# Linear attention and a GELU layer on one Trainium2 core: the order of all 3,662 operations comes from a table instead of a list scheduler

## The chip, the cores and the metric

The kernel runs on one core of a Trainium2 chip. A core has five engines, each of which takes its own instructions in order: TensorE (PE in the profile; its weight loads are shown as PEld), VectorE (DVE), ScalarE (ACT), GpSimd (POOL) and SyncE (SP, which issues nearly all DMA transfers). The metric is the device time of one execution in microseconds.

## The reference

```
def phi(x):
    proj = np.einsum('bhsd,df->bhsf', x, w_phi)
    proj = proj - np.max(np.abs(proj), axis=-1, keepdims=True)
    return np.concatenate([np.exp(proj), np.exp(-proj)], axis=-1)
q_p, k_p = (phi(q), phi(k))
kv = np.einsum('bhsf,bhsd->bhfd', k_p, v)
z = np.sum(k_p, axis=2)
num = np.einsum('bhsf,bhfd->bhsd', q_p, kv)
den = np.einsum('bhsf,bhf->bhs', q_p, z)[..., None] + 1e-06
x = (num / den), heads side by side: 4608 tokens x 512
h = x @ w_in                                          # 512 x 2048
out = (0.5 * h * (1.0 + erf(h / sqrt(2)))) @ w_out    # 2048 x 512
```

Batch and heads are 8 and 8, the sequence has 576 tokens, a head 64 numbers and 128 features. The weights of the layer arrive as float64.

## The kernel before, in words

**Attention** runs batch by batch (b = 0 to 7), two heads (a pair) at a time. `k_unit` and `k_quad` project keys on PE (tile `pk`, `pk_r` for the rest of a sequence), take the largest absolute value (`mx`, L465, DVE), subtract it (`ek` or `er`, L401, DVE) and exponentiate on ACT (L470); PE sums keys times values (`kv`), and ACT copies the sums out (`kvn`, L395). `q_pair` projects queries (`pq`), ACT copies them (`pc`), POOL finds the largest absolute value over the partitions (`mb`, L539), DVE subtracts it (`pc`, L401), ACT exponentiates twice (`ef`, L544), PE multiplies (`pn`, and for b under 3 the denominators `dn`), ACT copies the results (`xo`, `do`) and SP stores them. In what follows k10 is pair 0 of the keys of b = 1, and q001 is b = 0, pair 0, second half of the sequence; w_i0_0 and w_o1 are pieces of the two weights.

**Weights** are split from float64 into two float32r parts: 32 pieces of 128 x 512. Each piece (`split_weight`, L413 to L423) is a load of 512 KB (`raw`), an absolute value on ACT (L416, tile `wt`), four DVE instructions (L417, L419, L421, L423), a cast on ACT and a subtraction on DVE (L401, tile `w_i` or `w_o`).

**The layer** runs over 18 blocks of 256 tokens. `up` gives 12 matmuls per 128 hidden columns into `ph`; ACT applies GELU; DVE subtracts to get the low part (`gl`); the second product goes into `po`. Blocks 8 to 17 (`seven`) need fewer products (`pa`, `pb`).

All operations are recorded with `op` in `Plan.ops`, each with its engine, its dependencies and a rank. `Plan.order` then ran a list scheduler over them, with costs, latencies and a model of a few effects, and `emit` issued the operations by planned start. Tile places are fixed by name (`HOME`) and by each tag's own rotation. What counts on the chip is each engine's own sequence, since an engine never overtakes itself; SP's sequence is at once the order of the DMA transfers.

Of the kernel before, what the change touches and what calls it, by code (L numbers as in the profile page):

```python
# [62 lines left out]
class Plan:  # L63


    HOP = {"pe": 0.2, "act": 0.14, "dve": 0.13, "pool": 0.1, "sp": 0.05}
    SAME = {"pe": 0.0, "act": 0.0, "dve": 0.127, "pool": 0.1, "sp": 0.0}
    SWITCH = 1.3

    BEHIND = {"f": 0.1, "k": 0.1, "q": 0.095, "v": 0.09, "w": 0.09, "n": 0.1, "d": 0.05, "z": 0.09}  # L70
    BEFORE = {"f": 0.08, "k": 0.1, "q": 0.1, "v": 0.05, "w": 0.05, "n": 0.05, "d": 0.1, "z": 0.04}
    SHAPE = {"f": 0, "k": 1, "q": 1, "v": 2, "n": 2, "w": 3, "d": 4, "z": 5}
    READS = {"max": 1.15, "add": 2.45, "max main": 2.1, "add main": 4.43, "max rest": 1.05, "add rest": 2.15}
    WRITES = {"max": (1.4, 2.02), "add": (2.75, 3.47), "max main": (2.3, 3.42), "add main": (4.6, 5.97), "max rest": (1.2, 1.83), "add rest": (2.4, 3.1)}
    SPENT = {"max": 2.14, "add": 3.59, "max main": 3.54, "add main": 6.11, "max rest": 1.94, "add rest": 3.23}
    WINDOW = 3.413
    BUSY = 0.8
# [5 lines left out]

    def turn(self, a, b):
        return self.BEHIND[a] + self.BEFORE[b] + (0.09 if a == "f" and b != "d" else 0.0)

# [47 lines left out]
    def order(self, bias):  # L134
        free = dict(self.slots)
        slot_free_at = {t: [0.0] * n for t, n in self.slots.items()}
        turn = dict.fromkeys(self.slots, 0)
        engines = {}
        for o in self.ops:
            engines.setdefault(o.eng, [])  # L140
        clock = dict.fromkeys(engines, 0.0)
        table = [None]
        cand = {e: [] for e in engines}
        for o in self.ops:
            if o.wait == 0:
                cand[o.eng].append(o)
        done = []
        n = len(self.ops)

        gelus, left_at, dma, dge = [0], [0.0], [0.0], [0.9]  # L150
        port = [0.0]

        def start_of(o):
            t = max(clock[o.eng], o.ready)
            if o.table == "exp" and table[0] == "gelu" and gelus[0] % (2 * STICK):
                t = max(t, left_at[0] + PATIENCE)
            seen = {}
            for b in o.bufs:
                if not b.held and b.tag is not None:
                    f, i = slot_free_at[b.tag], seen.get(b.tag, 0)  # L160
                    if len(b.line) <= i or b.line[i] is not b:
                        return None
                    when = f[(turn[b.tag] + i) % len(f)]
                    if when is None:
                        return None
                    t = max(t, when)
                    seen[b.tag] = i + 1
            if o.eng == "dve":
                for a, z, least in port[1:]:
                    if o.port >= least and a <= t < z:  # L170
                        t = z
            return t


        clk = {"i": 0, "full": False, "busy": 0.0}
        last, first = ["f"], {}

        def run(t, work, duty):
            while work > 1e-9:
                i = int(t / self.WINDOW + 1e-9)  # L180
                while clk["i"] < i:
                    use = clk["busy"] / self.WINDOW
                    clk["full"] = use > (0.5 if clk["full"] else self.BUSY)
                    clk["i"] += 1
                    clk["busy"] = 0.0
                speed = 1.0 if clk["full"] else 0.51
                dt = min((i + 1) * self.WINDOW - t, work / speed)
                clk["busy"] += dt * duty
                work -= dt * speed
                t += dt  # L190
            return t

        while len(done) < n:
            best = None
            for e, lst in cand.items():
                if not lst:
                    continue
                opts = []
                for o in lst:
                    t = start_of(o)  # L200
                    if t is not None:
                        opts.append((t, o))
                if not opts:
                    continue
                t0 = min(t for t, _ in opts)
                lim = max(t0, clock[e]) + 0.02
                hold = 0.0
                if e == "pe" and last[0] == "f":
                    t_of = {id(o): max(o.ready, first.setdefault(o.n, t)) for t, o in opts}
                    there = [o for t, o in opts if t <= lim and o.kind != "f"]  # L210
                    if sum(o.cost for o in there) < LUMP and all(lim - t_of[id(o)] < LINGER for o in there):
                        hold = 4000.0
                key = None
                for t, o in opts:
                    if t <= lim:
                        k = o.rank
                        if e == "act" and o.table is not None and o.table != table[0]:
                            k += bias
                        if o.kind != "f":
                            k += hold  # L220
                        if key is None or (k, o.n) < key[0]:
                            key = ((k, o.n), t, o)
                if best is None or key[1] < best[1] or key[1] == best[1] and e == "pool":
                    best = key
            if best is None:
                raise RuntimeError("no operation can go")
            _, t, o = best
            cand[o.eng].remove(o)
            cost = o.cost
            if o.eng == "act" and o.table is not None and o.table != table[0]:  # L230
                cost += self.SWITCH
                table[0] = o.table
            if o.eng == "pe":
                if self.SHAPE[last[0]] != self.SHAPE[o.kind]:
                    cost += self.turn(last[0], o.kind)
                last[0] = o.kind
            o.start = t
            if o.eng == "pool" and o.port:
                t = max(t, port[0])
                a, z = self.WRITES[o.port]  # L240
                port[1:] = [(t, t + self.READS[o.port], 1), (t + a, t + z, 2)]
            o.end = run(t, cost, o.duty) if o.eng == "pe" else t + cost
            if o.nbytes:
                dge[0] = max(dge[0], t) + 0.55
                dma[0] = max(dma[0], dge[0] + 0.75) + o.nbytes / RATE
                o.late = dma[0] + 0.15 + DMASLACK - o.end
            if o.table == "gelu":
                gelus[0] += 1
                left_at[0] = o.end
            clock[o.eng] = o.end  # L250
            if o.eng == "dve" and o.port:
                port[0] = o.end
            for b in o.bufs:
                if b.tag is not None and not b.held:
                    f = slot_free_at[b.tag]
                    b.slot = turn[b.tag]
                    f[b.slot] = None
                    turn[b.tag] = (b.slot + 1) % len(f)
                    b.held = True
                    assert b.line.pop(0) is b  # L260
                b.left -= 1
                if b.left == 0 and b.tag is not None:
                    slot_free_at[b.tag][b.slot] = o.end + o.late + self.HOP[o.eng] + (PESLACK if b.tag in self.banks else 0.0)
            for u in o.users:
                u.wait -= 1
                u.ready = max(u.ready, o.end + o.late + (self.HOP if u.eng != o.eng else self.SAME)[o.eng] + (POOLSLACK if o.eng == "pool" else 0.0) + (PESLACK if u.eng == "pe" and o.eng != "pe" else 0.0))
                if u.wait == 0:
                    cand[u.eng].append(u)
            done.append(o)
        self.done = done  # L270
        return max(o.end + o.late for o in done)

    def emit(self):
        todo = sorted(self.done, key=lambda o: (o.start, o.n))
        parts = [o.part for o in todo if o.eng == "pe"][1:] + [None]
        for o in todo:
            if o.eng == "pe":
                self.then = parts.pop(0)
            if o.reopen and self.turn_over is not None:
                self.turn_over()  # L280
# [35 lines left out]
def fused_kernel(ctx: ExitStack, tc: tile.TileContext, qT, kT, va, w_st, w_in, w_out, out):  # L316
    nc = tc.nc
    plan = Plan(tc)
# [611 lines left out]
    total = plan.order(bias=BIAS)  # L930
# [155 lines left out]
```

## Time and profile before

| what | value |
|---|---|
| median of 3 runs | 1046.52 us (1044.51 to 1047.1) |
| profiled execution, its own time | 1048.43 us |
| span of its instructions | 1046.6 us |
| mean granted share of the TensorE clock | 0.993 |
| PE busy | 1019.6 us, 97% |
| DVE busy | 661.1 us, 63% |
| ACT busy | 614.5 us, 59% |
| POOL busy | 276.9 us, 26% |

Busy is the time in which an engine executes an instruction. Shares over the whole span hide stages: the page's 40 slices show DVE at nine tenths in the first eight slices and PE at nine tenths or more from the fifth on. A row of waits names who ended an idle stretch of an engine; a chain row is a piece of the path that ended last.

### The profile page before, as it was taken

The page shows a single profiled execution, that of the slowest core. Times are in us where ns is not written, and L with a number is a line of the kernel's source. Part 1 is how long each engine was busy: PE and PEld are TensorE (multiplying, and loading weights), DVE is VectorE, ACT ScalarE, POOL GpSimd, SP SyncE. Part 2 cuts the span into 40 slices and gives each one's busy share as a digit, 9 for nine tenths or more (in the row PEclk, how much of TensorE's full clock was granted, in tenths as well). Part 3 has the DMA queues.
Part 4 walks back from the last instruction along what each step waited for, and adds up shares of the span by engine and source line. Part 5 has one row for each costly group of instructions (what it writes and reads, how often), then busy time and mean ns, then how long its engine had stood idle before and what let it go on. Part 6 is the DMA issues. An engine that isn't in the chain of part 4 may idle for free.

```text
span 1046.6 us, 24197 instructions
## 1 busy us (share of the span) xinstructions
PE 1019.6 (97%) x10070; PEld 893.1 (85%) x10070; DVE 661.1 (63%) x1209; ACT 614.5 (59%) x1011; POOL 276.9 (26%) x72
## 2 busy tenths in 40 slices
PE   6889998999999999999999999999999999999998
PEld 5555776878878878897887889999999999999998
DVE  5899999987777854334643433555564556474754
ACT  5788888886768766757755642343243334243433
POOL 2343331373376352326566540000000000000000
PEclk9899999999999999999999999999999999999999
DMA  8775654524534433222321339201111111110000
GB/s 294 216 231 170 208 189 119 164 88 140 162 123 147 152 108 91 67 76 72 97 72 39 97 107 326 60 22 41 44 39 40 43 42 42 41 42 19 24 22 21
DMA packets 87327, 107.11 MB, mean 102 GB/s; under 512 B 29021, under 2 KB 57245, under 8 KB 87217
## 3 DMA queue, kind: packets, MB, share of 16 engines
q1 hardware_dynamic: 86928, 105.30, 32.7%
q8 instruction: 79, 1.29, 0.5%
q14 instruction: 32, 0.25, 0.1%
q10 hardware_dynamic: 288, 0.26, 0.1%
HBM read 75.87 MB, written 29.66 MB: 101 GB/s over the span
## 4 chain that ended last, share of the span: by engine, by line
PE 90%; DVE 5%; ACT 2%; issue 1%; DMA 1%; SPq 0%; DVEq 0%; ACTq 0%
PE ph L360 38%; PE po L360 17%; PE pa L360 10%; PE pb L360 7%; PE kv L360 6%; PE pn L360 4%; PE pk L360 3%; PE pq L360 3%; PE dn L360 1%; DVE wt_i L421 1%; PE pn_rest L360 1%; DMA vt<-in_va_dram 1%; DVE ek L401 0%; DVE wt_i L423 0%; DVE pc L401 0%
## 5 line engine op out<-in xcount | busy, mean ns | idle before, releaser
L360 PE MATMUL ph<-xh,w_i 128*128 128x256 f32 x2304 | 416.6, 278 | 0.0
L360 PEld LDWEIGHTS ph<-xh,w_i 128*128 128x128 f32 x2304 | 357.1, 188 | 9.0 <-issue 5.1
L360 PE MATMUL ph<-xl,w_i 128*128 128x256 f32 x1152 | 319.3, 277 | 0.0
L360 PEld LDWEIGHTS ph<-xl,w_i 128*128 128x128 f32 x1152 | 217.2, 189 | 0.3
L539 POOL PARTITION_ALL_REDUCE mb<-pc x36 | 120.6, 3356 | 202.3 <-ACT pc L395 153.3
L360 PE MATMUL po<-w_o,gh 128*128 128x512 f32 (+1 forms) x519 | 162.4, 395 | 0.0
L550 POOL PARTITION_ALL_REDUCE db<-pc x20 | 124.2, 6212 | 93.7 <-DVE pc L600 89.9
L360 PEld LDWEIGHTS po<-w_o,gh 128*128 128x128 f32 x519 | 93.3, 188 | 30.0 <-issue 8.5
L401 DVE TENSOR_TENSOR sg<-ga 128x256 f32<-128x256 f32 (+1 forms) x240 | 84.3, 376 | 54.1 <-ACT ga L839 50.3
L360 PE MATMUL pa<-w_o,oh 128*128 128x256 f32 x640 | 112.6, 276 | 0.0
L401 DVE TENSOR_TENSOR gl<-ph,gh 128x512 fp32r<-128x512 f32 x64 | 43.5, 687 | 90.7 <-ACT ph L750 90.6
L360 PE MATMUL po<-w_o,gl 128*128 128x512 f32 (+1 forms) x275 | 100.8, 378 | 0.0
L360 PEld LDWEIGHTS pa<-w_o,oh 128*128 128x128 f32 x640 | 96.3, 188 | 0.1
L839 ACT ACTIVATE ga<-ph 128x512 f32<-128x512 f32 x80 | 47.8, 597 | 82.3 <-PE ph L360 52.1
L401 DVE TENSOR_TENSOR ul<-sg,uh 128x384 fp32r<-128x384 f32 x80 | 44.6, 558 | 71.5 <-ACT uh L395 70.3
L360 PE MATMUL pa<-w_o,ol 128*128 128x256 f32 x320 | 88.3, 276 | 0.0
L360 PE MATMUL pb<-tw,uh 128*128 128x256 f32 x464 | 82.9, 276 | 0.1
L544 ACT ACTIVATE ef<-pc 128x1024 f32<-128x1024 f32 (+1 forms) x72 | 68.1, 973 | 14.2 <-DVE pc L401 10.3
L470 ACT ACTIVATE ek<-ek 128x1024 f32<-128x1024 f32 x64 | 67.6, 1059 | 11.1 <-DVE ek L401 10.2
L395 ACT CAST uh<-sg 128x384 fp32r<-128x384 f32 x80 | 41.0, 512 | 50.6 <-PE pb L360 25.3
L360 PEld LDWEIGHTS pb<-tw,uh 128*128 128x128 f32 x464 | 69.9, 188 | 0.3 <-DVE ob L401 0.3
L360 PE MATMUL pn<-ef,kvn 128*64 128x512 f32 (+1 forms) x288 | 64.9, 571 | 1.9 <-ACT do L395 0.8
(93 smaller groups left out, 1591.5 us busy)
## 6 DMA issues: line engine op xcount, KB each, us to landing
vt<-in_va_dram SPq DMA_DIRECT2D x32, 325.0 KB
t_d<-ts SPq DMA_DIRECT2D x40, 256.0 KB
out_dram<-ob SPq DMA_DIRECT2D x34, 256.0 KB
kt<-in_kT_dram SPq DMA_DIRECT2D x32, 256.0 KB
raw_i<-in_w_in_dram SPq DMA_DIRECT2D x16, 512.0 KB
raw_o<-in_w_out_dram SPq DMA_DIRECT2D x16, 512.0 KB
qt<-in_qT_dram SPq DMA_DIRECT2D x28, 256.0 KB
x_d<-xo SPq DMA_DIRECT2D x28, 256.0 KB
```

The costliest lines, as they stand in the source:

```text
L360: return tc.keep_in_program_order(nc.tensor.matmul(*a, **kw))
L395: op(eng, cost, lambda: nc.scalar.copy(out=dst(), in_=src()), r=r, w=w, **kw)
L401: op(eng, cost, lambda: e.tensor_tensor(out=dst(), in0=a(), in1=b(), op=o), r=r, w=w, **kw)
L421: op("dve", dve(512), lambda: v.scalar_tensor_tensor(out=t(), in0=low(), scalar=29, in1=t(), op0=ALU.logical_shift_right, op1=ALU.bitwise_ ...
L470: op("act", act(256 * n), lambda s=s: nc.scalar.activation(e[s](), e[1](), AF.Exp, scale=1.0 - 2.0 * s), r=[e[1]], w=[e[s]], table="exp", ...
L539: op("pool", plan.SPENT[most], lambda: nc.gpsimd.partition_all_reduce(mb(), pc(), P, bass_isa.ReduceOp.absmax), r=[pc], w=[mb], port=most, ...
L544: op("act", act(2 * n), lambda s=s: nc.scalar.activation(ef[s](), pc(), AF.Exp, scale=1.0 - 2.0 * s), r=[pc], w=[ef[s]], table="exp", **k())
L550: op("pool", plan.SPENT[total], lambda: nc.gpsimd.partition_all_reduce(db(), pc()[:, :2], P, bass_isa.ReduceOp.add), r=[pc], w=[db], port= ...
L839: op("act", act(2 * TB, True) + 0.037, lambda ph=ph, ga=ga: nc.scalar.activation(ga(), ph(), AF.Gelu), r=[ph_all], w=[ga], table="gelu", a ...
```

## The change

The scheduler in `Plan.order` goes, with its constants. The order is now a table, `ORDER`, of all operation numbers; `emit` follows it as it stands. Operations, tiles and their places are the same. Four constants that set the earliest planned start of some operations (`SUMSAT`, `SUMSEACH`, `WPACE`, `HOLD`) have other values, but nothing reads a planned start any more, and `DELAY`, which only moved ranks, is empty.

```
-    def order(self, bias):
-        free = dict(self.slots)
...
-        self.done = done
-        return max(o.end + o.late for o in done)
+    def order(self):
+        self.done = [self.ops[int(n)] for n in ORDER.split()]
+        assert len({o.n for o in self.done}) == len(self.ops)
 
     def emit(self):
-        todo = sorted(self.done, key=lambda o: (o.start, o.n))
+        todo = self.done
         parts = [o.part for o in todo if o.eng == "pe"][1:] + [None]
...
+ORDER = """
+3 0 30 2 9 1 4 45 13 58 157 27 5 11 6 71 10 7 165 46 14 15 47 48 29 8 59 158 60 16 61 17 159 31 205 12 20 160 161 28 466 32 229 173 18 49 50 21 51 162
...
```

Counted engine by engine against the sequence of before, 83 of 914 PE operations stand elsewhere, 207 of 1,209 on DVE, 181 of 933 on ACT, 198 of 538 on SP and 1 of 68 on POOL. On PE the last moved one is the 287th, so from there on PE's sequence is that of before. 24 of the groups of the second product (`po`) are issued as 6 matmuls instead of 7 or the other way round, since the split depends on what follows; that is 10 instructions more in all.

Three places, as the two programs list them. Line numbers differ (L563 became L414, L477 L328, L494 L345, L496 L347, L390 L241, L413 L264; L465 became L316, L401 L252, L417 to L423 L268 to L274). The number at a name's end only counts the tiles made.

SP at the start of the program, before: queries first, the small weight `wst` of the projections sixth.

```order
L563 DMA qt_0_0_1_114<-in_qT_dram 128x288
L563 DMA qt_0_1_1_116<-in_qT_dram 128x288
L477 DMA kr_0_118<-in_kT_dram 128x2x128
L563 DMA qt_0_1_0_120<-in_qT_dram 128x288
L563 DMA qt_0_0_0_122<-in_qT_dram 128x288
L390 DMA wst_124<-in_w_st_dram 128x128
L494 DMA kt_0_0_0_126<-in_kT_dram 128x512
L496 DMA vt_0_0_0_128<-in_va_dram 128x650
```

The same place now:

```order
L328 DMA kr_0_112<-in_kT_dram 128x2x128
L347 DMA vt_0_1_1_116<-in_va_dram 128x650
L241 DMA wst_118<-in_w_st_dram 128x128
L345 DMA kt_0_0_0_120<-in_kT_dram 128x512
L414 DMA qt_0_0_0_128<-in_qT_dram 128x288
L414 DMA qt_0_1_0_139<-in_qT_dram 128x288
L264 DMA raw_i0_0_141<-in_w_in_dram 128x512
L345 DMA kt_0_1_0_143<-in_kT_dram 128x512
```

`wst` went from sixth to third, the two queries of the second half left the front, and the first weight piece went from fifteenth to seventh.

DVE behind its first keys (k00), before:

```order
L401 TENSOR_TENSOR ek_0_0_0_1_181<-pk_0_0_0_156,mx_0_0_0_174 128x1024
L465 TENSOR_REDUCE mx_0_0_1_213<-pk_0_0_1_192 128x8
L401 TENSOR_TENSOR pc_0_0_0_179<-pc_0_0_0_179,mb_0_0_0_183 128x576
L465 TENSOR_REDUCE mx_0_1_0_259<-pk_0_1_0_204 128x8
L401 TENSOR_TENSOR pc_0_1_0_188<-pc_0_1_0_188,mb_0_1_0_201 128x576
```

The same place now:

```order
L252 TENSOR_TENSOR ek_0_0_0_1_164<-pk_0_0_0_130,mx_0_0_0_162 128x1024
L268 TENSOR_SCALAR wt_i0_0_176<-wt_i0_0_176 128x512
L270 TENSOR_SCALAR wt_i0_0_176<-wt_i0_0_176 128x512
L272 SCALAR_TENSOR_TENSOR wt_i0_0_176<-raw_i0_0_141,wt_i0_0_176 128x512
L316 TENSOR_REDUCE mx_0_1_0_214<-pk_0_1_0_186 128x8
L252 TENSOR_TENSOR pc_0_0_0_166<-pc_0_0_0_166,mb_0_0_0_168 128x576
```

Three instructions on the first weight piece came forward, and the keys k02 (`mx_0_1_0`) now precede k01 (`mx_0_0_1`), on PE too.

DVE ahead of the second piece of the second weight (w_o1), before:

```order
L421 SCALAR_TENSOR_TENSOR wt_o0_562<-raw_o0_298,wt_o0_562 128x512
L423 SCALAR_TENSOR_TENSOR wt_o0_562<-raw_o0_298,wt_o0_562 128x512
L417 TENSOR_SCALAR wt_o1_668<-wt_o1_668 128x512
L401 TENSOR_TENSOR pc_0_0_1_619<-pc_0_0_1_619,mb_0_0_1_635 128x576
L465 TENSOR_REDUCE mx_1_0_1_718<-pk_1_0_1_652 128x8
```

The same place now:

```order
L274 SCALAR_TENSOR_TENSOR wt_o0_567<-raw_o0_402,wt_o0_567 128x512
L252 TENSOR_TENSOR pc_0_0_1_611<-pc_0_0_1_611,mb_0_0_1_623 128x576
L316 TENSOR_REDUCE mx_1_0_1_716<-pk_1_0_1_628 128x8
L268 TENSOR_SCALAR wt_o1_697<-wt_o1_697 128x512
```

The query q001 and the keys k11 (`mx_1_0_1`) went ahead of the first instruction on w_o1. Further up, `mx` and `ek` of the keys k10 went from the 36th and 38th DVE instruction to the 32nd and 34th, past L419, L421 and L423 of the piece w_i3_0.

## Rows read from the trace of the kernel before

**Rows 1.** Stretches: length, busy us of each engine (instructions), PE clock, DMA share, GB/s.

```profile
core 0: us, PE busy (x) PEld busy (x) DVE busy (x) ACT busy (x) POOL busy (x), PEclk, DMA share, GB/s
...
0.00:170.00 170.00, 147.36 (x2101) 105.12 (x2102) 149.97 (x218) 135.38 (x215) 52.90 (x22) 0.96 0.67 214
170.00:1041.00 871.00, 870.85 (x7961) 786.79 (x7960) 508.46 (x985) 478.64 (x796) 224.04 (x50) 1.00 0.27 81
...
50.00:170.00 120.00, 110.53 (x1471) 76.78 (x1466) 114.81 (x171) 102.32 (x160) 40.75 (x13) 0.99 0.62 196
...
200.00:650.00 450.00, 450.00 (x4178) 371.17 (x4176) 259.55 (x376) 295.97 (x410) 215.98 (x48) 1.00 0.38 116
```

**Rows 2.** Chain that ended last, first 205 us: start, us, what.

```profile
3.09 3.08 DMA wst<-in_w_st_dram
...
125.97 1.22 DVE mx L465
...
169.52 5.64 PE ph L360 x48
```

**Rows 3.** Waits of DVE, 0 to 170 us: in total, times, longest.

```profile
DVE mx_r L465 <- PE pk_r L360: 6.2, 1, 6.2
DVE mx L465 <- PE pk L360: 4.8, 5, 2.5
DVE wt_o L417 <- ACT wt_o L416: 4.6, 3, 3.9
```

**Rows 4.** SP's first issues (timeline): start, us of issuing.

```profile
1.63 0.43 SPq L477 DMA_DIRECT2D kr<-in_kT_dram  x1
...
3.09 0.43 SPq L390 DMA_DIRECT2D wst<-in_w_st_dram  x1
```

**Rows 5.** DVE in order of time: start, us, [idle before, releaser].

```profile
14.25 1.22 DVE L465 TENSOR_REDUCE mx<-pk 128x8 f32<-128x1024 f32 x1 [2.49 <-PE pk L360]
15.39 0.75 DVE L401 TENSOR_TENSOR pc<-pc,mb 128x576 f32<-128x576 f32 x1
...
34.44 0.42 DVE L419 TENSOR_SCALAR wt_i<-wt_i 128x512 uint32<-128x512 uint32 x1
34.89 1.82 DVE L421 SCALAR_TENSOR_TENSOR wt_i<-raw_i,wt_i 128x512 uint32<-128x512 uint32 x1
36.74 0.69 DVE L423 SCALAR_TENSOR_TENSOR wt_i<-raw_i,wt_i 128x512 uint32<-128x512 uint32 x1
...
46.98 0.43 DVE L417 TENSOR_SCALAR wt_o<-wt_o 128x512 f32<-128x512 f32 x1 [3.89 <-ACT wt_o L416]
```

**Rows 6.** Waits of PE, 0 to 170 us: in total, times, longest.

```profile
PE dn L360 <- ACT xo L395: 3.0, 2, 1.7
PE pq L360 <- DVE ek L401: 3.0, 1, 3.0
PE kv L360 <- DMA vt<-in_va_dram: 2.3, 1, 2.3
PE dn L360 <- ACT do L395: 2.2, 1, 2.2
```

**Rows 7.** Stretches at the lower clock: columns as in rows 1.

```profile
12.70:16.10 3.40, 3.40 (x36) 3.18 (x34) 1.85 (x3) 1.65 (x2) 2.50 (x2) 0.50 1.03 393
...
40.00:46.80 6.80, 6.29 (x40) 3.46 (x42) 3.02 (x6) 4.80 (x8) 2.48 (x1) 0.50 0.73 214
...
84.40:87.80 3.40, 3.40 (x22) 2.67 (x14) 3.40 (x7) 2.77 (x4) 1.71 (x1) 0.50 0.68 180
```

**Rows 8.** The whole chain: two runs of 48 matmuls into ph.

```profile
537.64 5.44 PE ph L360 x48
...
548.61 5.66 PE ph L360 x48
```

**Rows 9.** DVE groups by shape, 0 to 170 us: count, busy us, mean ns.

```profile
L421 DVE SCALAR_TENSOR_TENSOR wt_o<-raw_o,wt_o 128x512 uint32<-128x512 uint32 x13 | 12.8, 985 | 0.1
...
L423 DVE SCALAR_TENSOR_TENSOR wt_o<-raw_o,wt_o 128x512 uint32<-128x512 uint32 x12 | 8.2, 684 | 0.1
```

More of the change, by code (lines that the diff above doesn't have):

```diff
@@ L63 @@
 class Plan:
[L66 to L74, printed above, removed]
     SPENT = {"max": 2.14, "add": 3.59, "max main": 3.54, "add main": 6.11, "max rest": 1.94, "add rest": 3.23}
-    WINDOW = 3.413
-    BUSY = 0.8
     def __init__(self, tc):
@@ L82, in __init__ @@
         self.tc, self.ops, self.slots, self.lines, self.stream, self.since, self.unit = tc, [], {}, {}, None, 0.0, "start"
-    def turn(self, a, b):
-        return self.BEHIND[a] + self.BEFORE[b] + (0.09 if a == "f" and b != "d" else 0.0)
     def pool(self, pool, tag, bufs):
@@ L132, in op @@
         return o
-    def order(self, bias):
-        free = dict(self.slots)
[L136 to L269, printed above, removed]
-        self.done = done
-        return max(o.end + o.late for o in done)
@@ L929, in fused_kernel @@
             seven(j, tw, lambda x, t=t, d=d: t + d * x, earlier if j == SEVEN else ())
-    total = plan.order(bias=BIAS)
-    if VERBOSE:
-        print("planned", total, {e: sum(o.cost for o in plan.done if o.eng == e) for e in ("pe", "dve", "act", "pool", "sp")})
+    plan.order()
     plan.emit()
-DELAY = {
[40 rows of a table removed]
-}
+DELAY = {}
 HOME = {
@@ L1012 @@
 SUMS = 2
-SUMSAT = 175.933
-SUMSEACH = 3.384
+SUMSAT = 190.75
+SUMSEACH = 4.989
 SUMSPAN = 581.86
@@ L1017 @@
 T18 = 997.68
-BIAS = 551.516
-STICK = 2
-PATIENCE = 2.138
 URGE = -1000.0
 EARLY = 41.32
-WPACE = 4.989
+WPACE = 4.81
 WSPAN = 48.9
@@ L1028 @@
 ND = 3
-LUMP = 82.289
-LINGER = 6.494
 PAIR_K = 0.224
@@ L1034 @@
 LEAD = 85.26
-HOLD = 23.07
+HOLD = 32.35
 WR = -23.78
@@ L1038 @@
 AT = 175.45
-PESLACK = 0.03
-POOLSLACK = 0.3
-DMASLACK = 0.517
 T0 = 85.1
-RATE = 285.0
-VERBOSE = False
+ORDER = """
[115 rows of a table added]
+"""
 _ARGS = ["qT", "kT", "va", "w_st", "w_in", "w_out"]
```

154 rows, old and new, of tables (DELAY, ORDER) are left out of this document.

## The prediction

> **What bounds the kernel now.** I read the stretches first, because the shares over the whole span say little [rows 1]. From 170 us to 1041 us PE is busy 870.85 of 871.00 us: there it is the bound and waits for nobody. In the first 170 us it is busy 147.36, so 22.6 us are idle, and nowhere else is there much to find but the first six microseconds of this same stretch and a tail of under 5 us. DVE is busy 149.97 us of those 170; from 50 us to 170 us it is busy 114.81 of 120, which is 96%. The chain of waits agrees: it runs from DVE's `mx` at 125.97 us through DVE and ACT, and settles on PE's layer work at 169.52 us [rows 2]. So the early stretch has a bound of its own, DVE, and whatever the early stretch saves arrives undiminished at the end if PE's work behind it stays closed. The waits of DVE say where its 20.0 idle microseconds lie: 6.2 until the first projection on PE is there, 4.8 for later projections, 4.6 for ACT's step on a weight piece [rows 3]; 0.9 is ahead of the program's first instruction, the rest is in pieces under 0.7 us.
>
> I therefore keep two accounts for the first 170 us, one of DVE and one of PE. The smaller saving is the one that counts.
>
> **DVE's account, step by step.**
>
> The start. The first projection waits for `wst`, issued at 3.09 us and landed 3.08 us later [rows 2]. In the new order it takes the third place on SP, that of 1.63 us [rows 4]. Moved by 1.46 us with the same time to landing, everything behind it starts 1.46 us sooner. The ends are 0 (the large load now ahead of it costs as much as the queries did) and 2.5 us (fewer bytes ahead); I take 1.46, the measured step of issues.
>
> The first hole. DVE idles 2.49 us ahead of the `mx` at 14.25 us [rows 5]. The new order puts L417, L419 and L421 of the first weight piece there. By the nearest rows of those shapes, 0.43, 0.42 and 0.69 us (the last from L423, which has the same shape and two operands too), that is 1.5 us of work that no longer stands in the closed part. Its load went from fifteenth to seventh on SP, so it should be there. Ends: 0 (the load lands late) and 2.49 (the hole closes wholly). I take 1.5.
>
> The second hole. DVE idles 3.89 us at 46.98 us for ACT's step on w_o1 [rows 5]. Now `pc` of q001 (0.75) and `mx` of k11 (1.22) stand ahead of that wait, which is 1.97 us of work in the hole. In the old sequence these two stood idle behind an instruction that they do not need. ACT itself gets to w_o1 sooner, since the copy `do` of q030 that stood just ahead of it came forward; I take 2.9, about midway between 1.97 and 3.89. The lower end is 0: if PE is late with k11, the wait only changes its name.
>
> The small holes. From 50 us to 170 us DVE idles 5.2 us [rows 1]. Half of them end with a late PE or ACT, which start sooner now; I take 2.6, ends 0 and 5.2.
>
> DVE's sum: 1.46 + 1.5 + 2.9 + 2.6 = 8.5 us. The amount of DVE work in front does not change it: `ek` of k30, on which the last key sums before PE closes rest, is the 201st DVE instruction before and the 197th now.
>
> **PE's account.** The first 170 us hold 22.6 us idle. They also hold three stretches at the lower of the two clock levels, 1.2 GHz, with 3.40, 6.29 and 3.40 us of PE work [rows 7]; at 2.4 GHz half of these 13.1 us would be saved, 6.5 us. The waits that the new order touches are these [rows 6]. `pq` waited 3.0 us for `ek` of k10; `ek` now stands ahead of L419, L421 and L423 of a weight piece, 0.42 + 1.82 + 0.69 = 2.9 us [rows 5], so this one goes. `dn` of q110 waited 2.2 us for a copy `do` on ACT that stood behind a cast, which in turn waited for DVE; the copy now precedes the cast, and PE has a query and a key projection in front of the first block's matmuls. I count both in full, the start with 1.46, half of the 3.0 us on `xo`, half of the 2.3 us on `vt` (its place is still freed by the key sums of k11, but fewer weight loads are queued beside it), and half of the clock's 6.5. That is 3.0 + 2.2 + 1.46 + 1.5 + 1.15 + 3.25 = 12.6 us. PE could save more than DVE gives, so DVE's 8.5 us decide, and PE closes at about 161 us instead of 169.5.
>
> **Behind 170 us.** PE's sequence changes up to its 287th operation. Leaving layer matmuls for attention and coming back costs little: 48 matmuls into `ph` take 5.44 us in one place and 5.66 where the shape has just changed [rows 8]. Of such crossings there are 52 among the operations from the 131st to the 300th before, 48 now, so 4 x 0.1 = 0.4 us less (0.22 for a way there and back). The ten additional `po` matmuls are halves of others and cost nothing that I can see; I leave them at 0, with 0.5 us as the other end. POOL's sequence swaps two neighbours, which ACT and DVE cover. The trace of before shows that DVE has room later: 259.55 of 450 us between 200 and 650 us [rows 1].
>
> A rule speaks against taking this stretch as closed. The Trainium skill, Perfetto Trace Analysis, section Identifying the Most-Contended Engine, calls matmul busy time a poor measure and weight-load busy time a good one. By it there would be 450 - 371.17 = 79 us of headroom left in the stretch from 200 to 650 us, and an order could draw on it. I go by the rows: each kind of operation there takes its own shortest time but for the 0.2 us at a change of shape.
>
> **Sum.** 8.5 + 0.4 = 8.9 us. Against the profiled execution: 1048.43 - 8.9 = 1039.5 us, of which the span is 1046.6 - 8.9 = 1037.7. The median of the runs shown is 1.91 us below that execution, so the forecast is 1046.52 - 8.9 = **1037.6 us**.
>
> **The rivals.**
>
> *Given back.* The start comes (1.46) and the first hole is used (1.5), but the second hole only changes its releaser and the small ones stay: 3.0 us, 1043.5 us. For it speaks that DVE is 96% busy behind 50 us, so that a saving there must come from somewhere else; against it that the two instructions which now fill the second hole need nothing from ACT's weight step. Chance 0.17, spread from 0 to 5 us of gain.
>
> *All holes close.* DVE's 20.0 us shrink to what the start must keep, 6.2 + 0.9 - 1.46 = 5.6 us. Gain 14.4 + 0.4: 1031.7 us. PE's account would then have to give more than 12.6, which it can only if the lower clock and the `vt` wait go wholly. Chance 0.07.
>
> *Denser PE behind 170 us*, the rule above at work: at most all 52 crossings x 0.11 = 5.7 us on top, 1031.9 us. The sequence keeps nearly all crossings, so chance 0.02.
>
> *Slower: DVE against POOL.* A DVE instruction that meets a POOL call can be held up: L421 took 1.82 us where its neighbour of the same shape took 0.69 [rows 5], and the 13 instructions of L421 on `wt_o` average 985 ns against 684 for L423 [rows 9], 3.9 us for this kind alone. POOL makes 22 calls of 52.90 us together in the first 170 us [rows 1]. The new order sets other DVE instructions beside these calls, and weight steps, the ones that are held up, came forward. At 1.13 us each, eight more hits take back 8.9 us, and eleven (12.4 us) give 1050.0 us. Against it: the same instructions, the same calls and the same sequence on POOL, so hits should change places rather than grow in number. Chance 0.05. The Trainium skill, SBUF — State Buffer, section Who interferes with whom, has these two engines share a port as an exclusive lock, the later one blocked for the whole instruction. By it a hit could cost a whole call, 52.90 / 22 = 2.4 us, and four more hits would decide; the rows show holds of 1 to 2 us, so I keep 1.13.
>
> **How the numbers follow.** About 0.3%, 3.1 us, is what a measurement of this kernel can tell from no change. The forecast (5 to 13 us of gain) has 0.69. Faster by over 3.1 us: the forecast, the two larger gains, and half of the rival that gives back: 0.69 + 0.07 + 0.02 + 0.09 = 0.87. Within 3.1 us: the other half, 0.08. Slower: 0.05. The range goes from all holes closed, rounded to 1031.5 us, to the gain that is given back, 1043.5 us.
>
> **What would show it.** In the new profile the first matmul should start soon after 3.09 + 3.08 - 1.46 = 4.7 us. DVE's idle time ahead of its sixth instruction and ahead of the first step on w_o1 should shrink to about 1 us each, and its busy share from 0 to 50 us rise from 149.97 - 114.81 = 35.2 us to over 40. PE should have no `pq` waiting for `ek` around 33 to 36 us, and should close near 161 us. From there to the end the length should be that of before. I am wrong if PE idles behind 200 us, if DVE's idle time up to PE's closing point stays near 20 us, or if DVE's mean durations beside POOL grow.

## The result and the profile after

| | before | changed |
|---|---|---|
| median (9 runs each) | 1047.1 us (1044.51 to 1049.8) | 1054.28 us (1050.31 to 1059.31) |
| ratio to before | | 1.0076, 95% interval 1.0055 to 1.0097 |
| profiled execution, its span | 1048.43, 1046.6 us | 1053.44, 1051.7 us |
| DVE busy | 661.1 us | 688.8 us, with the same 1,209 instructions |

The change makes the kernel slower by 0.76%. Forecast were 1037.6 us, 1031.5 to 1043.5.

In what follows b1_1 is step 1 of block 1 of the layer, counted from 0. Of line numbers now: L252 is the subtraction (L401 before), L246 the copy (L395), L316 `mx`, L451 the last step on `pc` ahead of the sum `db` over the partitions, L390 and L401 are POOL's two all-reduces (`mb`, `db`; L539 and L550 before).

The stretches first. Views of the changed kernel: length, busy us of each engine (instructions), clock, DMA share, GB/s.

```profile
0.00:170.00 170.00, 149.10 (x2117) 106.37 (x2118) 156.43 (x215) 134.19 (x214) 57.18 (x22) 0.97 0.67 211
170.00:1041.00 871.00, 866.16 (x7911) 781.95 (x7910) 527.21 (x981) 466.60 (x787) 223.37 (x50) 1.00 0.27 81
50.00:170.00 120.00, 109.21 (x1363) 74.75 (x1358) 114.57 (x160) 97.05 (x151) 42.44 (x12) 0.97 0.62 186
200.00:650.00 450.00, 446.22 (x4134) 367.27 (x4135) 276.88 (x377) 286.25 (x402) 213.65 (x48) 1.00 0.37 113
200.60:207.40 6.80, 3.91 (x21) 3.92 (x22) 5.88 (x6) 2.46 (x3) 3.46 (x1) 0.75 0.56 176
```

Against [rows 1] DVE is busier in the first 170 us (156.43 us for 215 instructions; it was 149.97 for 218), so its instructions have become longer. PE is no longer closed behind 170 us: 866.16 of 871. Between 200 and 650 us DVE needs 276.88 us for 377 instructions, where 376 took 259.55. The last row is a new gap: PE is busy 3.91 of 6.80 us, at a mean granted clock of 0.75, that is half of the stretch at 1.2 GHz.

The two spans differ by 5.1 us. PE's idle time gives 1.7 back in the first 170 us (22.6 before, 20.9 now) and costs 4.7 behind them (0.15 before, 4.84 now, both up to 1041 us); its busy time is 2.1 us longer (1021.7 against 1019.6).

The waits of PE up to 210 us (in total, times, longest):

```profile
PE pk_r L211 <- DMA wst<-in_w_st_dram: 4.8, 1, 4.8
PE ph L211 <- DVE gl L252: 4.4, 2, 3.5
PE pn L211 <- DVE gl L252: 2.9, 1, 2.9
PE po L211 <- DVE gl L252: 2.4, 1, 2.4
...
PE dn L211 <- ACT xo L246: 1.9, 3, 0.7
PE kv L211 <- DMA vt<-in_va_dram: 1.6, 2, 1.2
...
PE pq L211 <- DVE ek L252: 0.3, 1, 0.3
```

What the new order was to shorten is shorter: the start (6.3 before), `pq` for `ek` (3.0), `dn` for `xo` (3.0), `kv` for `vt` (2.3), and the wait of `dn` for `do` (2.2) has left the list [rows 6]. But PE now waits 9.7 us for `gl`, the low part of the GELU's result from DVE (4.4 + 2.9 + 2.4), which it never waited for before. Its wait for `kvn` has grown too, from 0.5 us to 2.0.

Where DVE lost time shows when both profiles are read up to the start of the same `gl`: first b0_0, then b1_1. The kernel before, then the changed one, columns as above (DVE's busy time is the third).

```profile
0.00:95.65 95.65, 76.03 (x1192) 54.81 (x1194) 78.25 (x104) 71.05 (x116) 33.73 (x16) 0.93 0.72 230
...
0.00:197.96 197.96, 175.32 (x2391) 128.27 (x2393) 176.94 (x260) 160.98 (x250) 60.69 (x24) 0.97 0.63 197
```

```profile
0.00:88.49 88.49, 73.54 (x1244) 54.05 (x1244) 80.03 (x101) 70.23 (x116) 34.33 (x16) 0.98 0.75 239
...
0.00:202.78 202.78, 178.20 (x2452) 130.55 (x2452) 188.39 (x257) 160.12 (x251) 69.68 (x25) 0.97 0.60 190
```

Up to b0_0 DVE is idle 88.49 - 80.03 = 8.5 us instead of 95.65 - 78.25 = 17.4, so 8.9 us have been gained; it is 7.2 us ahead. Up to b1_1 the idle time is 14.4 instead of 21.0 us, still 6.6 us better, but DVE has been busy 11.5 us longer with 3 instructions fewer, and the same `gl` starts 4.8 us late. The place itself, on DVE, POOL and PE of the changed kernel:

```profile
197.12 0.74 DVE L451 SCALAR_TENSOR_TENSOR pc<-ef,kvn,pc 128x512 f32<-128x512 f32 x1
197.97 4.79 DVE L252 TENSOR_TENSOR ts<-ts 128x256 fp32r<-128x256 f32 x1
202.69 0.17 DVE L517 RECIPROCAL dc<-dc 128x4 f32<-128x4 f32 x1
202.78 0.65 DVE L252 TENSOR_TENSOR gl<-ph,gh 128x512 fp32r<-128x512 f32 x1
```

```profile
197.95 6.11 POOL L401 PARTITION_ALL_REDUCE db<-pc  x1 [9.75 <-DVE pc L451]
```

```profile
203.49 0.58 PE L211 MATMUL ph<-xh,w_i 128*128 128x256 f32 x1 [3.51 <-DVE gl L252]
```

L451 releases POOL's all-reduce; the very next DVE instruction, a small subtraction that takes 0.4 us elsewhere, starts 0.02 us behind the call and takes 4.79. `gl` stands behind it, and PE behind `gl`. In the kernel before, the same release is followed by the `mx` of k33, which reads PSUM and keeps its 1.22 us:

```profile
198.90 0.74 DVE L600 SCALAR_TENSOR_TENSOR pc<-ef,kvn,pc 128x512 f32<-128x512 f32 x1
200.50 1.22 DVE L465 TENSOR_REDUCE mx<-pk 128x8 f32<-128x1024 f32 x1 [0.86 <-PE pk L360]
```

Call an instruction held if it takes over 0.25 us longer than the lower quartile of its form (the duration that a quarter of the instructions of the same line, tiles and shape stay under), and the surplus its hold. In the first 650 us 30 instructions are held before, for 39.3 us, and 44 now, for 65.8; up to the `gl` of b1_1 it is 14.9 us before and 26.2 now, 11.3 of the 11.5 us by which DVE is busy longer there. All of them run beside an all-reduce of POOL. Of the instructions that begin during one, those that read PSUM (`mx`, `ek`, `gl` and the rests `mx_r`, `er`) were never held, 0 of 72 before and 0 of 77 now; of the others 30 of 110 were, and now 44 of 114.

### The profile page after: what moved, and what is told of

Same layout as the page of the kernel before. It is cut to its first block, busy times and chain, and to the rows that moved or that the text cites. A ratio compares the mean times of both kernels' runs of the same rounds, so it can differ in the third digit from the quotient of the medians.

```text
span 1051.7 us, 24170 instructions
## 1 busy us (share of the span) xinstructions
PE 1021.7 (97%) x10080; PEld 894.5 (85%) x10080; DVE 688.8 (65%) x1209; ACT 603.4 (57%) x1007; POOL 280.5 (27%) x72
## 4 chain that ended last, share of the span: by engine, by line
PE 82%; DVE 9%; ACT 3%; issue 2%; DMA 1%; DVEq 0%; SPq 0%; ACTq 0%
PE ph L211 35%; PE po L211 16%; PE pa L211 10%; PE pb L211 7%; PE kv L211 4%; PE pn L211 4%; PE pq L211 2%; PE pk L211 2%; DVE ek L252 1%; DVE mx L316 1%; DVE xl L252 1%; DVE wt_i L268 1%; DVE pc L252 1%; DVE wt_o L272 1%; ACT ef L395 1%
## 5 line engine op out<-in xcount | busy, mean ns | idle before, releaser
L390 POOL PARTITION_ALL_REDUCE mb<-pc x36 | 124.1, 3451 | 190.7 <-ACT pc L246 137.2
L401 POOL PARTITION_ALL_REDUCE db<-pc x20 | 125.2, 6258 | 106.5 <-DVE pc L451 102.7
L252 DVE TENSOR_TENSOR sg<-ga 128x256 f32<-128x256 f32 (+1 forms) x240 | 84.3, 376 | 54.1 <-ACT ga L690 50.3
L252 DVE TENSOR_TENSOR ul<-sg,uh 128x384 fp32r<-128x384 f32 x80 | 44.6, 558 | 71.0 <-ACT uh L246 71.0
L252 DVE TENSOR_TENSOR gl<-ph,gh 128x512 fp32r<-128x512 f32 x64 | 43.6, 684 | 63.9 <-ACT ph L601 63.9
L395 ACT ACTIVATE ef<-pc 128x1024 f32<-128x1024 f32 (+1 forms) x72 | 68.0, 972 | 11.4 <-DVE pc L252 8.9
L246 ACT CAST uh<-sg 128x384 fp32r<-128x384 f32 x80 | 41.0, 512 | 50.3 <-PE pb L211 25.3
```

The source lines that it names most:

```text
L246: op(eng, cost, lambda: nc.scalar.copy(out=dst(), in_=src()), r=r, w=w, **kw)
L252: op(eng, cost, lambda: e.tensor_tensor(out=dst(), in0=a(), in1=b(), op=o), r=r, w=w, **kw)
L390: op("pool", plan.SPENT[most], lambda: nc.gpsimd.partition_all_reduce(mb(), pc(), P, bass_isa.ReduceOp.absmax), r=[pc], w=[mb], port=most, ...
L395: op("act", act(2 * n), lambda s=s: nc.scalar.activation(ef[s](), pc(), AF.Exp, scale=1.0 - 2.0 * s), r=[pc], w=[ef[s]], table="exp", **k())
L401: op("pool", plan.SPENT[total], lambda: nc.gpsimd.partition_all_reduce(db(), pc()[:, :2], P, bass_isa.ReduceOp.add), r=[pc], w=[db], port= ...
```

## The experiments

POOL's all-reduces number 68 in all; the 56 of two expectations are those of `mb` and `db` without the rests of the sequences, and all 68 are replaced there. Three theories. H: DVE instructions held up beside POOL's calls, ahead of a result that PE waits for, take the gain and more. O: the new sequence of DVE is worse in itself, too much work stands ahead of `gl`. L: POOL's calls matter by their length, as a delay in the chain of the queries, and the new order bears that delay less well. Where a diff below lists names such as `gl (b1_1)`, it shows an engine's sequence in words, with most of it left out (DVE's, unless ACT is named); `ORDER` itself holds only numbers.

**One `gl` moved.** The changed kernel, DVE at 197.97 us:

```diff
 L451 pc (q300)
+L252 gl (b1_1)
 L252 ts (the one that was held)
 L517 dc
-L252 gl (b1_1)
```

> The changed kernel with one DVE instruction moved: the `gl` of block 1, second 128-column step, goes ahead of the one `ts` that met the POOL call at 197.95 us and was held 4.38 us; PE then waited 3.5 us for that `gl` and ran 3 us at the lower clock. Theory H (DVE instructions held up beside POOL's calls, ahead of a result that PE waits for, cost the time): the 4.9 us that PE lost at this place come back, ratio to before 1.0076 - 0.0047 = 1.003, PE's lead over before stays near -0.5 us behind this place. Theory O (the new sequence of DVE is worse in itself: it puts too much work ahead of `gl`, whatever POOL does): one instruction moved past 0.4 us of work brings at most 0.4 us, ratio 1.007.

Measured: 1052.31 us, ratio 1.0051 (1.0031 to 1.0071). H's 1.003 lies just outside this interval, O's 1.007 inside, and the interval overlaps that of the changed kernel. At the place itself PE gained about 0.5 us (from the start of one `kv` to that of the next it took 14.75 us, 15.26 in the changed kernel). The rows say why (DVE, ACT, PE of this kernel):

```profile
194.96 0.69 DVE L252 TENSOR_TENSOR gl<-ph,gh 128x512 fp32r<-128x512 f32 x1 [0.60 <-ACT ph L601]
195.57 3.70 DVE L252 TENSOR_TENSOR ts<-ts 128x256 fp32r<-128x256 f32 x1
```

```profile
201.47 0.58 ACT L246 COPY ob<-po 128x512 f32<-128x512 f32 x1 [5.16 <-DMA t_d<-ts]
```

```profile
202.11 0.73 PE L211 MATMUL po<-w_o,gh 128*128 128x512 f32 x2 [2.60 <-ACT ob L246]
```

`gl` came free, but `ts` was still held, and `ts` lies in the tag from which ACT's `ob` takes its place: ACT waited 5.16 us for the store of `ts`, and PE 2.60 us for ACT. One held instruction has two ways to PE. This run alone does not part H from O.

**Three calls rearranged.** As above, and at two more calls of POOL:

```diff
+L316 mx, L252 ek (k21)
 L268 wt_i (held 1.98 us at 79.4)
-L316 mx, L252 ek (k21)
+L252 gl (b0_0)
 L252 pc (q130)
-L252 gl (b0_0)
...
+L252 gl (b0_4)
 L272 wt_o (held 1.99 us at 143.7)
-L252 gl (b0_4)
```

> The changed kernel with DVE rearranged at three POOL calls (78.7, 143.3 and 197.95 us): instructions that read PSUM and were ready (`mx`, `ek` of k21; `gl` of block 0, step 4; `gl` of block 1, step 1) go ahead of the SBUF instructions that were held, and the first `gl` goes ahead of `pc` of q130. Theory H: the PE waits of 2.9, 2.4 and 3.5 us for `gl` go, with two low-clock stretches behind them, some 9 to 11 us; ratio to before 0.997 to 0.999. Theory O: under 1.5 us, ratio 1.006 or more.

Measured: 1048.78 us, ratio 1.0015 (1.0001 to 1.0030). From 1.0076 that is 6.4 us back, by moving five instructions past a few others. O allowed 1.5. H's 9 to 11 are not reached, since the wait for `ob` stayed (2.6 us), with 1.8 us for `xo_rest` on ACT.

**POOL's calls made short, in both orders.**

```diff
-nc.gpsimd.partition_all_reduce(mb(), pc(), P, bass_isa.ReduceOp.absmax)
+nc.gpsimd.memset(mb(), 0.0)
...
-nc.gpsimd.partition_all_reduce(db(), pc()[:, :2], P, bass_isa.ReduceOp.add)
+nc.gpsimd.memset(db(), 1.0)
```

The sequence of the kernel before:

> The kernel before with POOL's 56 all-reduces replaced by short memsets of the same tiles: the largest absolute values of the queries and the sums of the denominators are left out. Both theories: no held DVE instructions; faster than before by the 14 us that DVE was held up to PE's closing point, less what PE cannot take: ratio 0.985 to 0.995.

The sequence of the changed kernel:

> The changed kernel with the same replacement of POOL's 56 all-reduces by short memsets (largest values of the queries and sums of the denominators are left out). Theory H: without holds the new order shows its shorter DVE idle time, 4 to 9 us faster than the kernel before with the same replacement. Theory O: still slower than that kernel, by 3 us or more.

Measured: 1039.48 us with the old order (ratio 0.9930, 0.9903 to 0.9957), 1033.55 us with the new one (0.9870, 0.9847 to 0.9894). Without the all-reduces the new order is 5.9 us faster than the old; with them it is 7.2 us slower. O is out: this sequence is the better one as soon as the all-reduces no longer hold DVE, and PE's wait for `gl` shrinks from 9.7 to 0.2 us. Busy time of the engines over the whole span, old order and new:

```profile
PE 1015.1 (98%) x10070; PEld 890.3 (86%) x10070; DVE 627.8 (61%) x1209; ACT 612.9 (59%) x1011; POOL 55.8 (5%) x72
```

```profile
PE 1014.6 (98%) x10080; PEld 890.7 (86%) x10080; DVE 630.6 (61%) x1209; ACT 603.2 (58%) x1007; POOL 57.2 (6%) x72
```

**POOL as long and as late, without the all-reduce.** Short calls also take a delay out of the queries' chain, which L would credit. So each call became a one-column copy that waits for the same tile, and then memsets.

```diff
+def busy_pool(dst, src, times):
+    first = nc.gpsimd.tensor_copy(out=dst()[:, :, :1], in_=src()[:, :2, :1])
+    return [first] + [nc.gpsimd.memset(dst(), 1.0) for _ in range(times)]
...
-nc.gpsimd.partition_all_reduce(mb(), pc(), P, bass_isa.ReduceOp.absmax)
+busy_pool(mb, pc, 4)
...
-nc.gpsimd.partition_all_reduce(db(), pc()[:, :2], P, bass_isa.ReduceOp.add)
+busy_pool(db, pc, 7)
```

> The kernel before with each all-reduce replaced by a one-column copy that waits for the same tile and 4 memsets (7 for the denominators): POOL is about as long and as late as before, but does not hold DVE if memsets do not; the largest values of the queries and the sums of the denominators are left out. It parts theory H from theory L (POOL's length as a delay of the queries' chain, not the holds, makes the new order slow). H: 2 to 6 us faster than the kernel before, as with short memsets. L: like the kernel before, within 2 us.

> The changed kernel with the same replacement as the run above (largest values of the queries and sums of the denominators are left out). H: 3 to 7 us faster than the run above, since the holds are gone and the delay of POOL's calls stays. L: 3 us or more slower than the run above, as the changed kernel is against the kernel before.

Measured: 1043.37 us with the old order (0.9968, 0.9951 to 0.9984), 1038.08 us with the new one (0.9908, 0.9883 to 0.9934). POOL is even busier than with its all-reduces (276.9 and 280.5 us), and the new order is 5.3 us faster; PE waits 1.2 us for `gl`. L is out. Busy time, old order and new:

```profile
PE 1016.6 (98%) x10070; PEld 890.5 (86%) x10070; DVE 632.6 (61%) x1209; ACT 613.7 (59%) x1011; POOL 316.1 (30%) x419
```

```profile
PE 1015.9 (98%) x10080; PEld 890.4 (86%) x10080; DVE 636.5 (61%) x1209; ACT 603.8 (58%) x1007; POOL 320.8 (31%) x419
```

This pair also prices what the all-reduces hold beyond what memsets do: 661.1 - 632.6 = 28.5 us of DVE's busy time in the kernel before, 688.8 - 636.5 = 52.3 us in the changed one. The new order nearly doubles it.

It is not the whole price, since memsets hold DVE too, other instructions and for shorter: 14 of them for 9.3 us in the old order, 24 for 13.2 us in the new one (39.3 - 9.3 = 30.0 and 65.8 - 13.2 = 52.6, close to the two differences). All of these read one whole tensor from SBUF, most of all the step `pc<-ef,kvn` (`kvn` gives it one number per row). The first row is of the kernel before, the second of its order with the memsets:

```profile
L597 DVE TENSOR_SCALAR pc<-ef,kvn 128x512 f32<-128x512 f32 x40 | 21.4, 559 | 18.0 <-ACT ef L544 18.0
L451 DVE TENSOR_SCALAR pc<-ef,kvn 128x512 f32<-128x512 f32 x40 | 25.9, 673 | 13.2 <-ACT ef L398 13.2
```

So H is shown for the all-reduces, as against memsets of their length; a kernel in which nothing holds DVE was not run.

**Seven places.** The kernel of three calls, with four more:

```diff
 L451 pc (q300, first)
+L252 ts, L252 gl (b1_1)
 L451 pc (q300, second: releases the call)
-L252 gl (b1_1), L252 ts
...
+L252 gl (b1_0), L316 mx, L252 ek (k32)
 L252 ts (held 1.87 us at 179.7)
-L316 mx, L252 gl (b1_0), L252 ek (k32)
...
+L316 mx, L252 ek (k60), L252 gl (b4_1)
 L252 xl (held 4.0 us at 392.4)
-L316 mx, L252 ek (k60), L252 gl (b4_1)
...
+L246 do, L246 xo_rest (ACT)
 L267 wt_i (ACT)
-L246 do, L246 xo_rest (ACT)
```

> The kernel of the three rearranged calls with four more places rearranged: at 196.3 us the `ts` and the `gl` go ahead of the instruction that releases the POOL call (in the two runs before, the held `ts` kept its place in the tag that ACT's `ob` needs, and PE waited 2.6 us for that); at 179.7 us `gl`, `mx` and `ek` go ahead of the held `ts`; at 391 us `mx`, `ek` and `gl` go ahead of `xl`, held 4.0 us; and on ACT the copies `do` and `xo_rest` go ahead of the absolute value of a weight piece that waited for DVE. Theory H: the 2.8, 1.6, 2.0 and 2.0 us that PE loses at these places, 8.4 us, come back at least by half: ratio to before 0.992 to 0.998. Theory O: within 1 us of the kernel with three, ratio 1.0005 or more. If holds only change their places: 0.998 to 1.002.

Measured: 1043.66 us, ratio 0.9964 (0.9950 to 0.9978): within H's figure, 10.6 us under the changed kernel and clear of the kernel before. The last of the four places moves ACT's copies and stands at no POOL call; what it gives by itself was not measured. DVE at the place that lost 4.8 us:

```profile
191.50 0.43 DVE L252 TENSOR_TENSOR ts<-ts 128x256 fp32r<-128x256 f32 x1 [0.77 <-ACT ts L246]
191.99 0.69 DVE L252 TENSOR_TENSOR gl<-ph,gh 128x512 fp32r<-128x512 f32 x1
192.59 0.74 DVE L451 SCALAR_TENSOR_TENSOR pc<-ef,kvn,pc 128x512 f32<-128x512 f32 x1
...
193.34 1.19 DVE L316 TENSOR_REDUCE mx<-pk 128x8 f32<-128x1024 f32 x1
194.57 1.23 DVE L252 TENSOR_TENSOR ek<-pk,mx 128x1024 f32<-128x1024 f32 x1
195.71 2.80 DVE L252 TENSOR_TENSOR ts<-w_o,w_o 128x512 f32<-128x512 f32 x1
```

`ts` and `gl` are through before L451 releases the call (it runs from 193.43 us), `mx` and `ek` read PSUM and are not held, and the hold falls on an instruction that PE does not wait for.

The engines' busy time with seven:

```profile
PE 1017.4 (98%) x10080; PEld 891.8 (86%) x10080; DVE 681.7 (65%) x1209; ACT 604.8 (58%) x1007; POOL 281.1 (27%) x72
```

The holds have not gone: 42 instructions, 58.3 us, more than the 30 and 39.3 of the kernel before, which is slower. So their number does not decide the time; what PE waits for does. And a gap of PE costs more than its length: of the 10.9 us between the spans of the changed kernel and of this one (1051.7 and 1040.8), 4.3 are PE's own busy time (1021.7 and 1017.4). The changed kernel has four stretches of 3.4 us at 1.2 GHz, each behind a gap of PE; this one has none between 14 and 1041 us (granted clock 1.00).

**Nine and ten places.** Two more `gl` forward (b0_2, b0_5), then a third (b0_3):

```diff
+L252 gl (b0_2)
 L274 wt_i
 L252 pc (q200)
 L268 wt_i
-L252 gl (b0_2)
...
+L252 gl (b0_5)
 L272 wt_o
...
-L252 gl (b0_5)
```

> The kernel of the seven places with two more `gl` moved forward on DVE: block 0, step 2, ahead of the weight instruction at 110.0 us (it was ready at 109.4 and ran at 112.1; PE waited 1.45 us and then had a stretch of slow matmuls), and block 0, step 5, ahead of the weight instruction that met the POOL call at 140.3 us (ready at 140.1, ran at 144.0; PE waited 1.19 us). Theory H: 1.5 to 3.5 us faster than the kernel with seven, ratio to before 0.993 to 0.995. If the holds only move on: 0.9955 to 0.998.

```diff
+L252 gl (b0_3)
 L252 xr
 L272 wt_i
...
-L252 gl (b0_3)
```

> The kernel of the nine places with the `gl` of block 0, step 3, moved ahead of `xr` on DVE: in that run `xr` met the POOL call at about 113 us, was held 2.0 us (3.21 against 1.22), and PE waited 2.8 us for this `gl`; in the kernel of seven the same `xr` began 0.4 us later against its call and was not held, and the call took 7.2 us instead. Theory H: `gl` reads PSUM and is ready at 113.3, so it runs beside the call and PE's 2.8 us go: 1.5 to 4 us faster than the kernel of nine, ratio to before 0.993 to 0.9955. If the hold finds another instruction that PE needs: 0.996 to 0.999.

Measured: nine 1044.16 us, 0.9968 (0.9954 to 0.9982); ten 1042.53 us, 0.9958 (0.9942 to 0.9973). The kernel of nine is no faster than that of seven: the case "the holds only move on". DVE and POOL with seven, with nine and with ten:

```profile
113.62 1.22 DVE L252 TENSOR_TENSOR xr<-xr,xh 128x1024 f32<-128x1024 f32 x1
```

```profile
112.84 7.20 POOL L390 PARTITION_ALL_REDUCE mb<-pc  x1 [6.61 <-ACT pc L246]
```

```profile
113.22 3.21 DVE L252 TENSOR_TENSOR xr<-xr,xh 128x1024 f32<-128x1024 f32 x1
```

```profile
112.92 3.79 POOL L390 PARTITION_ALL_REDUCE mb<-pc  x1 [7.21 <-ACT pc L246]
```

```profile
113.19 0.69 DVE L252 TENSOR_TENSOR gl<-ph,gh 128x512 fp32r<-128x512 f32 x1
113.80 2.47 DVE L252 TENSOR_TENSOR xr<-xr,xh 128x1024 f32<-128x1024 f32 x1
```

With seven, `xr` begins 0.78 us behind the start of its call, is not held, and the call itself takes 7.20 us, about twice the 3.54 of an undisturbed one. With nine both start within 0.4 us of where they did, `xr` is held 2.0 us, and the call is short. With ten `gl` runs untouched beside the call and `xr`, which PE does not wait for, is held 1.25 us. From nine to ten it is 1.6 us by the medians and 1.0 by the ratios, where H had 1.5 to 4; H's range of ratios, 0.993 to 0.9955, was just missed. By their intervals seven, nine and ten cannot be told apart; each beats both kernels.

## Why the prediction was wrong

By its own steps:

- **The start**: right. PE's first wait is 4.8 us instead of 6.3, a gain of 1.5 for 1.46 forecast.
- **The first hole**: filled as forecast, and worth nothing. Two of the three weight instructions in it met a POOL call (DVE of the changed kernel; the calls run from 9.80 and from 12.03 us):

```profile
11.41 0.99 DVE L270 TENSOR_SCALAR wt_i<-wt_i 128x512 uint32<-128x512 uint32 x1
12.44 1.66 DVE L272 SCALAR_TENSOR_TENSOR wt_i<-raw_i,wt_i 128x512 uint32<-128x512 uint32 x1
14.02 1.21 DVE L316 TENSOR_REDUCE mx<-pk 128x8 f32<-128x1024 f32 x1
```

  They took 0.99 and 1.66 us where I had priced 0.42 and 0.69: 1.5 us of holds for 1.5 us of work.
- **The second hole**: right in size. DVE's waits for ACT's step on `wt_o` fell from 4.6 to 1.8 us.
- **The small holes**: not right. From 50 to 170 us DVE idles 5.4 us, where it was 5.2 and half was to go. Over the first 170 us its idle time fell by 6.5 us (20.0 to 13.6), for 8.5 forecast, and its busy time rose by the same 6.5 us (149.97 to 156.43): the whole saving went into longer instructions.
- **PE's account**: its waits for `ek` and `do` went as forecast, those for `xo` and `vt` shrank by somewhat less (1.1 for 1.5 us, 0.7 for 1.15). Of the clock it got nothing: 13.6 us of stretches at the lower level before, and four of 3.4 us now, at other places, each behind a gap of PE that is new or has grown, of 2.0 (for `kvn`), 2.9, 2.4 and 3.5 us (for `gl`). So of 12.6 us PE's idle time in these 170 us gave 1.7.
- **What failed** is a term that stood in the sum as nothing: the time for which DVE is held. I had it as the rival "DVE against POOL" and dismissed it with "hits should change places rather than grow in number", at 1.13 us each and a chance of 0.05. The runs show both halves of that wrong. The number grew, from 30 to 44 in the first 650 us. And a hold is not 1.13 us: it lasts until the call lets DVE go, up to 2.0 us in a call of 3.5 to 4.3 us, 4.4 in one of 6.1. 1.13 us came from one hit in a short call [rows 5].
- **"From there to the end the length should be that of before"** failed with it. I took the stretch from 200 us on as closed, with room on DVE [rows 1], and did not look at DVE's order there. The largest single loss stands at 198 us.

The rival's own point was eleven more hits, 12.4 us, for 1050.0 us. It was the right mechanism, and 0.05 was far too little for it. That DVE had 11.5 us more busy time at b1_1 matches its 12.4 by luck, though: its sum of hits times a price does not give the time, since the kernel of seven is held more than the kernel before and is faster.

Could it have been seen? In part from the order, which lists what follows each instruction that releases a POOL call. In the two executions the first DVE instruction to begin after the start of a call reads PSUM at 44 of 68 calls before and at 38 now. The code that the change removes says it more plainly, and I passed over it. `READS` in the old scheduler gives each kind of all-reduce a stretch from its start, 2.1 us for most `mb` and 4.43 for most `db`, in which no DVE operation is planned to start that has a `port`; `mx`, `ek` and `gl` have none. The hold of `ts` beside `db` measured 4.38 us. So the old order was made with these holds in view. That the holds grew because this went is likely and not shown: no run puts the model back.

The Trainium skill, SBUF — State Buffer, section Who interferes with whom, says which instructions to look for: a DVE instruction with at most one input in SBUF, outside the modes that use two ports, does not contend with GpSimd, and one with two inputs there contends only with a GpSimd instruction that reads SBUF. I had used that section for a price and not for this list. The traces agree with both halves: no reader of PSUM was held (0 of 149), and beside memsets, which only write, the `ts` with 256 fp32r columns keeps 420 ns on average, against 550 before and 629 now with the all-reduces. They disagree on the price that the prediction quotes: the lock is not held for the whole call, since `ts` was let go 4.8 us into one of 6.11 us. The steps on one tensor that the memsets hold fall under the first half only if they use one port, and no trace shows which they use.

Shown by runs: that the all-reduces turn a gain of 5 to 6 us into a loss of 7; that their delay is not the cause; that moving a few instructions, nearly all of them at the calls, brings back 10.6 us. Not shown: how the 7 us split over the single holds. Each moves all later ones, as the run with nine places shows, so they cannot be priced one by one.

## What to carry to other kernels

Where two engines can hold each other up, an order is not judged by idle time alone: list what stands behind each instruction that releases a call of the other engine, and put there what cannot be held, or what nobody waits for. To part an order's worth from such holds, replace the calls by work as long that takes less of what they share, in both orders, and count what is still held; the sign of the difference can turn over. When a scheduler goes, read what it had a model of: its order may owe something to it. And a held instruction is followed on all its ways, through the place its tile occupies too.

## What was not expected of the hardware

- Which of the two engines is held can turn over with a shift of 0.4 us: the same `xr` beside the same call lost nothing while the call grew to 7.20 us, then lost 2.0 us while the call took 3.79. What decides it I did not measure; it is not the distance alone, since with ten `xr` begins 1.04 us behind its call and is held. With seven the call began during the first of these two rows of DVE and ended 3.48 us behind the start of the second:

```profile
112.68 0.42 DVE L270 TENSOR_SCALAR wt_i<-wt_i 128x512 uint32<-128x512 uint32 x1
...
116.56 0.69 DVE L252 TENSOR_TENSOR gl<-ph,gh 128x512 fp32r<-128x512 f32 x1
```

  The six instructions from L270 to the one ahead of `gl` take their data from SBUF and follow each other without a pause, and 3.48 us is about a whole undisturbed call: it looks as if the call waited for the first reader of PSUM. With nine it did not: the call began during an instruction of that kind as well, and the next one, `xr`, was held. Why one and not the other stays open.
- The executions of the changed kernel spread over 9 us (1050.31 to 1059.31), those of the new order without all-reduces over 2.5 and 0.8 us (1032.05 to 1034.56 and 1037.73 to 1038.56, four executions each). The holds alone do not explain that: with seven nearly as many instructions are held, and twelve executions lie within 1042.23 to 1044.9. The reason stays open.
- The kernel before loses by holds too: 39.3 us of DVE's time, and with memsets in the place of its all-reduces it is 3.6 us faster.
